# Softmax reciprocals of every chunk by way of DRAM, one matmul group kept a tile behind another, and two small matmul groups joined, in a fused attention and gated-MLP kernel

## Chip, cores, metric

One core of a Trainium2 chip. The time is the device time in microseconds (us). The profile is of one execution of each kernel (230.45 us before), and its span (first to last instruction) is about 2 us shorter than the device time.

## The reference

```python
# x: [1, 2048, 512] bf16; 32 heads of 16; window of 8 taps, dilation 2
xn = layernorm(x)
q, k, v = split(xn @ wqkv)
logits[w] = sum_d q[s] * k[s - 2*w] / 4            # 8 taps, masked for s - 2w < 0
o = sum_w softmax(logits)[w] * v[s - 2*w]
s = o @ wo
y = (gelu(xn @ w_gate) * (xn @ w_up)) @ w_down     # hidden size 1792
return x + s * silu(y)
```

## The kernel before

The 2048 positions are worked in four chunks of 512. A chunk goes through "glu" (14 slots of a gate and an up projection, 4 matmuls each), then, for the next chunk, "qkv" (12 projections of 4 matmuls), then "down" (4 tiles of 128 positions: 14 matmuls for y, 4 for s). The attention of a chunk is hung between these on a list of places: VectorE makes products q*k (`pk`), TensorE sums them to logits `L` with a 32-column operand, ScalarE takes exp (`E`), VectorE makes products E*v (`pv`), and TensorE sums them over the taps (`o`). The denominators are a small sum of E alone; their reciprocals must be spread from 32 heads to 128 partitions before `o` is divided.

```python
    def denominators(j):                # 8 matmuls, 32 columns wide
        den = mm.tile([P, P], F32, name="den_ps", tag="mm")
        ...                             # lhsT=hsum, rhs=E
        nc.vector.reciprocal(out=rs[:], in_=den[:])

    def spread_reciprocals(j):          # last chunk only: 4 matmuls and an eviction
        sp = mm.tile([P, TQ], F32, name="sp_ps", tag="mm")
        for q in range(4):
            nc.tensor.matmul(sp[:, q * P : (q + 1) * P], lhsT=spread[:, q, :],
                             rhs=st[j]["rs"][:], start=True, stop=True)
        rb = op.tile([P, TQ], F32, name="rb")
        nc.scalar.activation(out=rb[:], in_=sp[:], func=AF.Copy)

    def spread_by_dma(j):               # the other chunks: store, then four reloads
        nc.sync.dma_start(out=rs_d[j][:, :], in_=st[j]["rs"][:])
        rb = op.tile([P, TQ], BF16, name="rbd")
        for i in range(WL):
            nc.sync.dma_start(out=rb[H * i : H * (i + 1), :]..., in_=rs_d[j]...)

    def av_sums(j): ...                 # 32 matmuls, 32 columns wide: o_ps <- pv
    def divide(j): ...                  # oT <- o_ps * rb, two VectorE operations

    def down(j, tt):
        y = mm.tile(...)                # 14 matmuls
        nc.scalar.activation(out=sl[:, cols], in_=y[:], func=AF.Silu)
        s = mm.tile(...)                # 4 matmuls, lhsT = oT
        nc.vector.tensor_tensor(out=m[:], in0=s[:], in1=sl[:, cols], op=ALU.mult)
        nc.vector.tensor_tensor(out=o_t[:, cols], in0=m[:], in1=x_sb[:, t, cols], op=ALU.add)
        nc.sync.dma_start(out=out2d[...], in_=o_t[:, cols])
    ...
    # places of chunk 0's attention (cut)
    at(("qkv", 1, 3), denominators, 0)
    at(("qkv", 1, 3), spread_by_dma, 0)
    at(("qkv", 1, 10), av_sums, 0)
    at(("qkv", 1, 10), divide, 0)
    ...
    # and of the last chunk
            at(("glu", j, 12), spread_reciprocals, j)
            at(("glu", j, 13), divide, j)
```

PSUM has four rotating buffers (`mm`) and one of four banks (`att`) for L and o in turn. All DMA is issued in order from one queue.

The softmax here doesn't subtract the row's maximum and nothing guards it: scores larger than these inputs give would overflow.

## Time and profile before

| | before |
|---|---|
| median of 3 runs | 230.13 us (230.06 to 230.57) |
| profiled span | 228.7 us |
| TensorE busy | 223.6 us (98%) |
| VectorE, ScalarE, GpSimd busy | 147.6, 130.2, 23.0 us |
| granted TensorE clock | 1.000 |

A busy TensorE is not one at full rate, so this goes by start to start: the difference between two starts in the PE timeline, divided by the matmuls in between, against the 0.216 us of a full-rate stretch. The lines are in the prediction.

### The profile page before, as it was taken

How to read it: one execution, taken by the hardware profiler on the slowest of the kernel's cores; microseconds unless marked ns; L12 is line 12 of the kernel's file. 1: busy time of each engine (PE TensorE's matmuls, PEld its weight loads, DVE VectorE, ACT ScalarE, POOL GpSimd, SP SyncE). 2: the span in 40 equal slices, each digit the busy share in tenths (PEclk: the TensorE clock that was granted, in tenths of full speed). 3: DMA queues.
4: the chain of work that ended last, by engine and by line, in shares of the span. 5: the costliest groups of instructions: out<-in, count | busy, mean ns of one | idle time of the engine just before them, and what ended most of it. 6: DMA issues, size and time to landing. Idle time of an engine off the chain costs nothing.

```text
span 228.7 us, 3538 instructions
## 1 busy us (share of the span) xinstructions
PE 223.6 (98%) x1324; PEld 106.3 (46%) x1324; DVE 147.6 (65%) x234; ACT 130.2 (57%) x214; POOL 23.0 (10%) x61
## 2 busy tenths in 40 slices
PE   8899999999999999999999999999999999999993
PEld 6764444444444444444444444444444444444453
DVE  4584996896995198865677169735549429945232
ACT  4679769764413866467621786747642396748211
POOL 1048973000000000110000000000000000000000
PEclk9999999999999999999999999999999999999999
DMA  6999589982378211110275711110147800000001
GB/s 163 359 373 371 140 170 199 242 204 75 109 172 197 55 24 29 26 29 0 92 175 135 170 25 28 26 34 0 45 120 165 203 26 3 0 0 4 23 23 46
DMA packets 30545, 24.46 MB, mean 107 GB/s; under 512 B 10176, under 2 KB 30528, under 8 KB 30528
## 3 DMA queue, kind: packets, MB, share of 16 engines
q1 hardware_dynamic: 30528, 24.24, 41.9%
q8 instruction: 10, 0.16, 0.3%
q14 instruction: 7, 0.06, 0.1%
HBM read 18.61 MB, written 4.31 MB: 100 GB/s over the span
## 4 chain that ended last, share of the span: by engine, by line
PE 94%; DMA 2%; ACT 1%; SPq 1%; DVE 0%; issue 0%; DVEq 0%
PE y_ps L416 21%; PE u_ps L247 21%; PE g_ps L247 21%; PE qkv_ps L247 17%; PE s_ps L426 6%; PE L_ps L304 3%; PE o_ps L375 3%; DMA wqkv_sb<-in_A_wqkv_dram 2%; PE q_ps L247 1%; ACT L400 1%; SPq L85 1%; PE den_ps L324 0%; ACT ge L400 0%; ACT vst L271 0%; PE tr L212 0%; ACT xnT L221 0%
## 5 line engine op out<-in xcount | busy, mean ns | idle before, releaser
L247 PE MATMUL g_ps<-xnT,wg_sb 128*128 128x512 bf16 x224 | 57.6, 379 | 0.0
L247 PE MATMUL u_ps<-xnT,wu_sb 128*128 128x512 bf16 x224 | 57.5, 379 | 0.0
L416 PE MATMUL y_ps<-wd_sb,h 128*128 128x512 bf16 (+1 forms) x238 | 51.2, 366 | 0.0
L404 DVE TENSOR_TENSOR h<-ge,u 128x512 bf16<-128x512 bf16 x56 | 23.8, 425 | 37.1 <-ACT u L402 36.4
L293 DVE TENSOR_TENSOR pk<-q_sb,k_sb 128x2048 bf16<-128x2048 bf16 x32 | 37.8, 1221 | 7.0 <-ACT k_sb L268 7.0
L402 ACT ACTIVATE u<-u_ps 128x512 bf16<-128x512 f32 x56 | 33.5, 599 | 14.7 <-PE u_ps L247 14.7
L400 ACT ACTIVATE ge<-g_ps 128x512 bf16<-128x512 f32 x56 | 33.5, 599 | 14.7 <-PE g_ps L247 14.4
L247 PE MATMUL qkv_ps<-xnT,wqkv_sb 128*128 128x512 bf16 (+1 forms) x208 | 40.9, 355 | 0.0
L361 DVE TENSOR_TENSOR pv<-E,v_arr 128x2048 bf16<-128x2048 bf16 x32 | 38.6, 1216 | 0.0
L416 PEld LDWEIGHTS <-h 128*128 128x128 bf16 x238 | 23.3, 98 | 25.3
L423 ACT ACTIVATE sl<-y_ps 128x512 bf16<-128x512 f32 (+1 forms) x17 | 9.7, 572 | 44.0 <-PE y_ps L416 44.0
L247 PEld LDWEIGHTS <-wu_sb 128*128 128x128 bf16 x224 | 21.9, 98 | 26.7 <-issue 0.3
L247 PEld LDWEIGHTS <-wg_sb 128*128 128x128 bf16 x224 | 21.2, 98 | 27.1 <-issue 3.0
L247 PEld LDWEIGHTS <-wqkv_sb 128*128 128x128 bf16 x224 | 21.6, 98 | 20.2 <-DMA wqkv_sb<-in_A_wqkv_dram 0.9
L434 DVE TENSOR_TENSOR m<-s_ps,sl 128x512 bf16<-128x512 f32 (+1 forms) x17 | 11.2, 658 | 24.2 <-PE s_ps L426 24.1
L426 PE MATMUL s_ps<-wo_sb,oT 128*128 128x512 bf16 (+1 forms) x68 | 16.6, 366 | 0.0
L197 POOL TENSOR_TENSOR rstd<-rstd,mhalf 128x1 f32<-128x1 f32 x12 | 7.7, 638 | 77.4 <-DVE rstd L194 75.2
L271 ACT ACTIVATE vst<-qkv_ps 128x512 bf16<-128x512 f32 x16 | 9.6, 597 | 6.4 <-PE qkv_ps L247 6.4
L268 ACT ACTIVATE k_sb<-qkv_ps 128x512 bf16<-128x512 f32 (+1 forms) x20 | 10.2, 514 | 3.5 <-PE qkv_ps L247 3.2
L265 ACT ACTIVATE q_sb<-qkv_ps 128x512 bf16<-128x512 f32 (+1 forms) x16 | 8.7, 544 | 3.6 <-PE qkv_ps L247 3.3
L426 PEld LDWEIGHTS <-oT 128*128 128x128 bf16 x68 | 6.6, 98 | 7.2
L159 POOL COPY spread<-ident 32x32 bf16<-32x32 bf16 x16 | 9.7, 646 | 0.2
(52 smaller groups left out, 115.8 us busy)
## 6 DMA issues: line engine op xcount, KB each, us to landing
v_arr<-vT SPq DMA_DIRECT2D x16, 520.0 KB, 5.1
vT<-vst SPq DMA_DIRECT2D x16, 128.0 KB, 2.1
out_dram<-o_t SPq DMA_DIRECT2D x15, 128.0 KB, 2.3
wg_sb<-in_B_w_gate_dram SPq DMA_DIRECT2D x2, 896.0 KB, 10.9
wu_sb<-in_B_w_up_dram SPq DMA_DIRECT2D x2, 896.0 KB, 12.7
wd_sb<-in_B_w_down_dram SPq DMA_DIRECT2D x1, 1792.0 KB, 13.7
wqkv_sb<-in_A_wqkv_dram SPq DMA_DIRECT2D x3, 512.0 KB, 5.6
x_sb<-in_A_x_dram SPq DMA_DIRECT2D x3, 512.0 KB, 11.4
```

The lines of the kernel that those rows point to most:

```text
L159: nc.gpsimd.tensor_copy(out=spread[H * q : H * (q + 1), q, H * j : H * (j + 1)], in_=ident[H * q : H * (q + 1), H * q : H * (q + 1)],)
L247: nc.tensor.matmul(ps, lhsT=w[:, dk, lo : lo + P], rhs=xnT[j][:, dk, i0 : i0 + n], start=(dk == 0), stop=(dk == NC - 1),)
L268: nc.scalar.activation(out=k_sb[:, c, lo : lo + n], in_=ps, func=AF.Copy)
L293: nc.vector.tensor_tensor(out=pk[:], in0=st[j]["q"][:], in1=k_sb[:, :, off : off + TQ], op=ALU.mult)
L361: nc.vector.tensor_tensor(out=pv[:], in0=st[j]["E"][:, wh, :].unsqueeze(1).to_broadcast([P, 4, TQ]), in1=st[j]["va"][:, 4 * g : 4 * g + 4, ...
L400: nc.scalar.activation(out=ge[:], in_=g_ps[:], func=AF.Gelu_apprx_tanh)
L402: nc.scalar.activation(out=u[:], in_=u_ps[:], func=AF.Copy)
L404: nc.vector.tensor_tensor(out=h[:], in0=ge[:], in1=u[:], op=ALU.mult)
L416: nc.tensor.matmul(y[:], lhsT=st[j][fc][:, tt * P : (tt + 1) * P], rhs=wd_sb[:, fc, cols], start=(fc == 0), stop=(fc == NF - 1),)
L423: nc.scalar.activation(out=sl[:, cols], in_=y[:], func=AF.Silu)
L426: nc.tensor.matmul(s[:], lhsT=st[j]["oT"][:, g, tt * P : (tt + 1) * P], rhs=wo_sb[:, g, cols], start=(g == 0), stop=(g == NC - 1),)
L434: nc.vector.tensor_tensor(out=m[:], in0=s[:], in1=sl[:, cols], op=ALU.mult)
```

## The change

The intent: take the last spread off TensorE, make one narrow group of chunk 0 out of two, and buy time for the divides that then come later by letting s run one tile behind y.

```diff
-    at(("qkv", 1, 3), denominators, 0)
-    at(("qkv", 1, 3), spread_by_dma, 0)
-    at(("qkv", 1, 10), av_sums, 0)
-    at(("qkv", 1, 10), divide, 0)
+    at(("qkv", 1, 8), denominators, 0)
+    at(("qkv", 1, 8), av_sums, 0)
+    at(("qkv", 1, 8), store_reciprocals, 0)
+    at(("qkv", 1, 10), spread_reciprocals, 0)     # now the DRAM way, for every chunk
+    at(("down", 0, 0), divide, 0)
...
-        if j + 1 < NJ:
-            at(("glu", j, 11), spread_by_dma, j)
-            at(("qkv", j + 1, 6), divide, j)
-        else:
-            at(("glu", j, 12), spread_reciprocals, j)
-            at(("glu", j, 13), divide, j)
+        at(("glu", j, 11), store_reciprocals, j)
+        at(("glu", j, 11), spread_reciprocals, j)
+        at(("qkv", j + 1, 6) if j + 1 < NJ else ("down", j, 0), divide, j)
...
-            down(j, tt)                            # y, then s of the same tile
+                sl = down(j, tt, cols)             # y
+                if todo:
+                    finish(*todo.pop())            # s of the tile before
+                if last:
+                    finish(j, tt, cols, sl)
+                else:
+                    todo.append((j, tt, cols, sl))
```

Cut: the constant `spread` and its 17 GpSimd instructions go; chunk 0's av products start one slot earlier; three products q*k of chunk 1 move ahead of chunk 0's y; `sl`, the silu of y, which now has to outlive the next y, gets three buffers in place of two.

More of the change, by code (lines that the diff above doesn't have):

```diff
@@ L81 @@
     vT = dram.tile([D, SV], BF16, name="vT")
-    rs_d = [dram.tile([P, P], BF16, name=f"rs_d{j}") for j in range(NJ - 1)]
+    rs_d = [dram.tile([P, P], BF16, name=f"rs_d{j}") for j in range(NJ)]
     def load_x(t, n=1):
@@ L140 @@
     hsum = const.tile([P, H], BF16, name="hsum")
-    spread = const.tile([P, 4, P], BF16, name="spread")
     dsum = const.tile([P, NC, H], BF16, name="dsum")
@@ L155, in sum_constants @@
             )
-        nc.gpsimd.memset(spread[:], 0.0)
-        for q in range(4):
-            for j in range(4):
-                nc.gpsimd.tensor_copy(
-                    out=spread[H * q : H * (q + 1), q, H * j : H * (j + 1)],
-                    in_=ident[H * q : H * (q + 1), H * q : H * (q + 1)],
-                )
     xnT = {}
@@ L334, in denominators, with store_reciprocals @@
         st[j]["rs"] = rs
+    def store_reciprocals(j):
+        nc.sync.dma_start(out=rs_d[j][:, :], in_=st[j]["rs"][:])
     def spread_reciprocals(j):
-        sp = mm.tile([P, TQ], F32, name="sp_ps", tag="mm")
-        for q in range(4):
-            nc.tensor.matmul(
-                sp[:, q * P : (q + 1) * P], lhsT=spread[:, q, :], rhs=st[j]["rs"][:],
-                start=True, stop=True,
-            )
-        rb = op.tile([P, TQ], F32, name="rb")
-        nc.scalar.activation(out=rb[:], in_=sp[:], func=AF.Copy)
-        st[j]["rb"] = rb
-    def spread_by_dma(j):
-        nc.sync.dma_start(out=rs_d[j][:, :], in_=st[j]["rs"][:])
-        rb = op.tile([P, TQ], BF16, name="rbd")
+        rb = op.tile([P, TQ], BF16, name="rb")
         for i in range(WL):
@@ L405, in glu @@
         st[j][fc] = h
-    def down(j, tt):
-        t = j * TPQ + tt
-        halves = [slice(0, D // 2), slice(D // 2, D)] if t == NT - 1 else [slice(0, D)]
-        n = D // len(halves)
-        sl = sm2.tile([P, D], BF16, name="sl")
-        o_t = sm4.tile([P, D], BF16, name="o_t")
-        for i, cols in enumerate(halves):
-            y = mm.tile([P, n], F32, name="y_ps", tag="mm")
-            for fc in range(NF):
-                nc.tensor.matmul(
-                    y[:],
-                    lhsT=st[j][fc][:, tt * P : (tt + 1) * P],
-                    rhs=wd_sb[:, fc, cols],
-                    start=(fc == 0),
-                    stop=(fc == NF - 1),
-                )
-            nc.scalar.activation(out=sl[:, cols], in_=y[:], func=AF.Silu)
-            s = mm.tile([P, n], F32, name="s_ps", tag="mm")
-            for g in range(NC):
-                nc.tensor.matmul(
-                    s[:],
-                    lhsT=st[j]["oT"][:, g, tt * P : (tt + 1) * P],
-                    rhs=wo_sb[:, g, cols],
-                    start=(g == 0),
-                    stop=(g == NC - 1),
-                )
-            m = sm2.tile([P, n], BF16, name="m")
-            nc.vector.tensor_tensor(out=m[:], in0=s[:], in1=sl[:, cols], op=ALU.mult)
-            nc.vector.tensor_tensor(out=o_t[:, cols], in0=m[:], in1=x_sb[:, t, cols], op=ALU.add)
-            nc.sync.dma_start(out=out2d[t * P : (t + 1) * P, cols], in_=o_t[:, cols])
@@ new lines, in down @@
+    def down(j, tt, cols):
+        n = cols.stop - cols.start
+        y = mm.tile([P, n], F32, name="y_ps", tag="mm")
+        for fc in range(NF):
+            nc.tensor.matmul(
+                y[:],
+                lhsT=st[j][fc][:, tt * P : (tt + 1) * P],
+                rhs=wd_sb[:, fc, cols],
+                start=(fc == 0),
+                stop=(fc == NF - 1),
+            )
+        sl = sm.tile([P, n], BF16, name="sl")
+        nc.scalar.activation(out=sl[:], in_=y[:], func=AF.Silu)
+        return sl
@@ new lines, in finish @@
+    def finish(j, tt, cols, sl):
+        t, n = j * TPQ + tt, cols.stop - cols.start
+        s = mm.tile([P, n], F32, name="s_ps", tag="mm")
+        for g in range(NC):
+            nc.tensor.matmul(
+                s[:],
+                lhsT=st[j]["oT"][:, g, tt * P : (tt + 1) * P],
+                rhs=wo_sb[:, g, cols],
+                start=(g == 0),
+                stop=(g == NC - 1),
+            )
+        m = sm2.tile([P, n], BF16, name="m")
+        nc.vector.tensor_tensor(out=m[:], in0=s[:], in1=sl[:], op=ALU.mult)
+        o_t = sm4.tile([P, n], BF16, name="o_t")
+        nc.vector.tensor_tensor(out=o_t[:], in0=m[:], in1=x_sb[:, t, cols], op=ALU.add)
+        nc.sync.dma_start(out=out2d[t * P : (t + 1) * P, cols], in_=o_t[:])
@@ L462 @@
     for i in range(8):
-        at(("glu", 0, 12 + i) if i < 2 else ("qkv", 1, (0, 1, 3, 4, 5, 6)[i - 2]),
+        at(("glu", 0, 11 + i) if i < 3 else ("qkv", 1, (0, 1, 2, 4, 5)[i - 3]),
            av_product, 0, i // 2, i % 2)
-    at(("qkv", 1, 3), denominators, 0)
-    at(("qkv", 1, 3), spread_by_dma, 0)
-    at(("qkv", 1, 10), av_sums, 0)
-    at(("qkv", 1, 10), divide, 0)
+    at(("qkv", 1, 8), denominators, 0)
[3 more added lines that the diff above has]
+    at(("down", 0, 0), divide, 0)
     for j in range(1, NJ):
         for w in range(W):
-            early = j > 1 and w < 3
-            at(("qkv", j, 9 + w) if early else ("down", j - 1, w // 3), qk_product, j, w)
+            at(("qkv", j, 9 + w) if w < 3 else ("down", j - 1, w // 3), qk_product, j, w)
         for i in range(TPQ):
@@ L538 @@
                 qkv(j + 1, i)
+        todo = []
         for tt in range(TPQ):
             run("down", j, tt)
-            down(j, tt)
+            last = j * TPQ + tt == NT - 1
+            for cols in (slice(0, D // 2), slice(D // 2, D)) if last else (slice(0, D),):
+                sl = down(j, tt, cols)
[5 more added lines that the diff above has]
+                    todo.append((j, tt, cols, sl))
+        if todo:
+            finish(*todo.pop())
 _INS = ['A_x', 'A_wqkv', 'A_wo', 'B_x', 'B_w_gate', 'B_w_up', 'B_w_down']
```

## The prediction

> **What bounds the kernel now.** I read the page first (busy shares, slices, chain), then the timeline of the TensorE, then the other engines' timelines around each instruction that moves. Busy shares and the chain of the page:
>
> ```profile
> PE 223.6 (98%) x1324; PEld 106.3 (46%) x1324; DVE 147.6 (65%) x234; ACT 130.2 (57%) x214; POOL 23.0 (10%) x61
> PE   8899999999999999999999999999999999999993
> ...
> PEclk9999999999999999999999999999999999999999
> ...
> PE 94%; DMA 2%; ACT 1%; SPq 1%; DVE 0%; issue 0%; DVEq 0%
> ```
>
> The TensorE (PE) is busy in every slice but the first two and the last, its clock is full, and 94% of the chain that ended last is PE. Busy is no proof of full rate, so I look at start to start in the PE timeline (start, duration, line, operation, count). These are chunk 0's attention among the projections of chunk 1, the same place in chunk 1 itself, the projections of chunk 2, and the spread in the last chunk:
>
> ```profile
> 44.75 2.75 PE L247 MATMUL qkv_ps<-xnT,wqkv_sb 128*128 128x512 bf16 x12
> 47.43 0.29 PE L324 MATMUL den_ps<-E,hsum 128*32 128x128 bf16 x8
> 47.66 6.22 PE L247 MATMUL qkv_ps<-xnT,wqkv_sb 128*128 128x512 bf16 x28
> 53.80 1.91 PE L375 MATMUL o_ps<-pv,hsum 128*32 128x512 bf16 x32
> 55.65 1.90 PE L247 MATMUL qkv_ps<-xnT,wqkv_sb 128*128 128x512 bf16 x8
> 57.38 3.18 PE L416 MATMUL y_ps<-wd_sb,h 128*128 128x512 bf16 x14
> 60.41 1.03 PE L426 MATMUL s_ps<-wo_sb,oT 128*128 128x512 bf16 x4
> 61.27 3.18 PE L416 MATMUL y_ps<-wd_sb,h 128*128 128x512 bf16 x14
> ...
> 93.00 1.03 PE L247 MATMUL u_ps<-xnT,wu_sb 128*128 128x512 bf16 x4
> 93.96 0.29 PE L324 MATMUL den_ps<-E,hsum 128*32 128x128 bf16 x8
> 94.08 1.90 PE L375 MATMUL o_ps<-pv,hsum 128*32 128x512 bf16 x32
> 95.91 1.04 PE L247 MATMUL g_ps<-xnT,wg_sb 128*128 128x512 bf16 x4
> ...
> 101.10 10.52 PE L247 MATMUL qkv_ps<-xnT,wqkv_sb 128*128 128x512 bf16 x48
> 111.46 3.19 PE L416 MATMUL y_ps<-wd_sb,h 128*128 128x512 bf16 x14
> ...
> 205.80 0.39 PE L339 MATMUL sp_ps<-rs,spread 128*128 128x128 bf16 x4
> 206.02 1.03 PE L247 MATMUL g_ps<-xnT,wg_sb 128*128 128x512 bf16 x4
> ```
>
> From 101.10 to 111.46 there are 48 matmuls: 10.36/48 = 0.216 us each. y takes 60.41 - 57.38 = 3.03 = 14 x 0.216, s takes 61.27 - 60.41 = 0.86 = 4 x 0.216. So PE runs y, s, y, s with no hole: s already finds its divided operand oT ready, and nothing in this pair is waiting today. Apart from the first 7 us and one hole of 0.2 us at 21.2 (ScalarE loading a table), the only PE time that is not streaming is about 0.1 us wherever the width of the stationary operand changes (128 to 32 columns or back): 55.65 - 53.80 is 1.85 for work that, four narrow matmuls side by side, streams in 8 x 0.216 = 1.73.
>
> **What the Trainium skill says.** "TensorE: Matmul & The Clock Gate", section "Wait — 56ns, not 53.3ns?": 512 columns back to back take 215.7 ns on a warm array; the trace's 0.216 us agrees, so these stretches have nothing left to give but instructions. "TensorEngine Tiling (Array Packing)", "Key Properties": changing the tiling mode drains the engine; the trace agrees with the 0.1 us above. "DMA: Bandwidth & Descriptors", "Anatomy of one DMA — SWDGE (gpsimd) path": a fixed cost of some 2.0 us per transfer, mostly waiting for the write to be confirmed. That fit is for another issuing path; in this trace the 32 KB stores of reciprocals land in 1.5 us (median) and their reloads in 1.7 us, so it is near, and the measured ones are used. "SBUF — State Buffer", "Who interferes with whom": a VectorE (DVE) operation with two SBUF inputs shuts out a GpSimd instruction that reads SBUF. The trace agrees: the 32x32 copies into `spread`, beside DVE's products, average 646 ns, the same copies into `hsum`, with DVE idle, 204 ns.
>
> **The change, part by part.**
>
> (1) The last chunk's spread goes by way of DRAM. It takes 4 matmuls off PE: 206.02 - 205.80 = 0.22 us, on the path, saved. It also takes one 0.59 us eviction off ScalarE and 17 instructions (9.7 + 0.5 = 10.2 us, 21 to 31.5 us) off GpSimd. ScalarE waits for PE before nearly every eviction at that place, GpSimd's next job comes at 33 us, and DVE's products took 1.22 us beside the copies and after them: off the path, worth 0. What it adds is a latency. In the last chunk the reciprocal ends at 203.25 + 0.95 = 204.2; store 1.5, four issues of 0.43, landing 1.7 of the last: about 204.2 + 1.5 + 1.3 + 1.7 = 208.7, 209 with the hand-overs. The divide now stands behind the last h product instead of before it: u of that product was evicted at 209.74 + 0.60, now 0.22 earlier, so h is done near 210.5. The two divides, 2.35 together, end at 212.9. s of tile 0 follows two y: 209.26 + 6.04 = 215.3. Slack 2.4 us: hidden.
>
> (2) Denominators of chunk 0 joined to the sums. Both use the same narrow operand, so one pair of changes of width goes. Apart: from 44.75 to 47.66 less 12 matmuls is 2.91 - 2.59 = 0.32, and 47.66 to 55.65 less 28 is 7.99 - 6.04 = 1.95; together 2.27. Joined, as in chunk 1: 93.00 to 95.91 less 4 matmuls is 2.91 - 0.86 = 2.05. Saved: 0.22 us on the path.
>
> (3) s one tile behind y. The same 14- and 4-matmul groups in another order, all 128 wide: 0 on PE. It loosens s's need of oT by 3.0 us in each chunk, which today nobody waits for. It serves to pay for (1) and for chunk 0's later divide. The tail stays y half, s half, m, o_t, store. Tile 2's s now ends 2.4 us before the end of PE, and its two DVE steps (0.69 + 0.42) and the first half's (0.42 + 0.29) fit in that: 1.82. So 0.
>
> (4) The sums of chunk 0 come two projections earlier, the av products one slot earlier, three products qk of chunk 1 earlier. This is the place to check; the DVE timeline in chunk 0:
>
> ```profile
> 43.30 1.22 DVE L361 TENSOR_TENSOR pv<-E,v_arr 128x2048 bf16<-128x2048 bf16 x1
> ...
> 49.65 0.95 DVE L333 RECIPROCAL rs<-den_ps 128x128 bf16<-128x128 f32 x1
> 50.51 3.43 DVE L361 TENSOR_TENSOR pv<-E,v_arr 128x2048 bf16<-128x2048 bf16 x3
> 55.77 2.36 DVE L387 TENSOR_TENSOR oT<-o_ps,rbd 128x1024 bf16<-128x1024 f32 x2 [1.83 <-PE o_ps L375]
> ```
>
> DVE runs without a hole from 42.6 to the last av product at 50.51 + 3.43 = 53.94. In the changed order the reciprocal (50.51 - 49.65 = 0.86) comes after it instead, so it ends at 53.08. PE reaches the sums after 8 projections: 44.75 + 32 x 0.216 = 51.66, denominators until 51.87, sums from there, eight steps of 0.216; the last product is needed at 51.87 + 7 x 0.216 = 53.38. Slack 0.3 us less a hand-over of 0.1: the narrowest point of the change.
>
> Chunk 0's divide: the reciprocal ends at 53.95, its store has landed at 55.6; the queue issues two stores of v in between (they wait for their evictions, to about 56.2), then four reloads to 58.4, the last landing near 59.7. The divide runs from 59.8 to 62.2. y starts at 57.16, so s of tile 0 starts at 57.16 + 6.04 = 63.2. Slack 1.0 us. After it DVE has five products and two m/o_t pairs, 5 x 1.14 + 2 x 1.05 = 7.8: 70.0, and the logits want the products at about 72.6.
>
> Sum: 0.22 + 0.22 = 0.44; 230.13 - 0.44 = 229.7.
>
> **Rivals.**
> (a) The sums of chunk 0 wait for the last av product. For: slack is 0.2 to 0.3 us, in an estimate as coarse as that. Against: the products' pace is steady to 0.01 us, and v_arr's last part lands at 30.1 + 12.1 = 42.2, before the earlier start of 42.96. If it misses by 0.2 to 0.5, half or all of the gain goes: 229.9 to 230.2.
> (b) Chunk 0's reloads of the reciprocals come late, because they queue behind stores of v (in the kernel before, two of those took 4 us to land when they stood behind the reloads). At 2 us later s would wait about 1 us: 230.7. Against: the v stores are issued 0.4 us or more ahead and are single ones.
> (c) The order y, y, s matters after all, because a PSUM buffer, ScalarE or DVE is freed sooner: 229.0 or less. Against: PE shows no hole at any y or s in the kernel before. A hole that does not exist cannot be filled.
> (d) The stores at the end bunch up (three within 2 us instead of 3.6) and the last one lands later by a few tenths: 229.9. Against: each is at most 128 KB and they are issued over 1 us apart or nearly so.
>
> **Range and chances.** All four rivals but (c) lead upwards by tenths, and the before runs themselves lie from 230.06 to 230.57. So 229.7, eight times in ten within 229.3 to 230.3. Two per cent is 4.6 us; only 0.44 us of work is removed, and no wait stands on PE that could give the rest: faster by over 2% has 1%. Slower by over 2% would need (b) several times over: 1%. Within 2%: 98%.
>
> **What would show it.** PE's timeline: no spread matmuls in the last chunk and its first y about 0.44 us earlier than 209.48; denominators and sums of chunk 0 in a row and y of chunk 0 near 57.16 instead of 57.38, a saving that stays constant until the last chunk. PE busy falls by about 0.4 us, instructions by 8 PE ones in all counting weight loads. A wait of PE for a pv or oT, which the kernel before does not have, would show (a) or (b); a first divide of chunk 0 later than 62 us, or a step in the saving at 63 us, would name (b). A saving above 0.7 us would mean that I overlooked a wait in the y and s pairs; a shorter PE but the same span would be (d).

## The result, and the profile after

229.75 us, median of 6 runs (229.62 to 229.99), against 230.12 us, median of 6 runs of the kernel before (229.93 to 230.57). The ratio is 0.9981, 95% interval 0.9968 to 0.9994: faster by 0.2%. (A ratio here is worked out from the fast runs of both kernels; it is not quite the ratio of the medians.)

The PE timeline of the changed kernel, same places as in the prediction (start, duration, line, operation, count):

```profile
44.54 7.07 PE L238 MATMUL qkv_ps<-xnT,wqkv_sb 128*128 128x512 bf16 x31
51.54 0.29 PE L315 MATMUL den_ps<-E,hsum 128*32 128x128 bf16 x8
51.66 1.90 PE L357 MATMUL o_ps<-pv,hsum 128*32 128x512 bf16 x32
53.49 3.63 PE L238 MATMUL qkv_ps<-xnT,wqkv_sb 128*128 128x512 bf16 x15
56.96 6.21 PE L394 MATMUL y_ps<-wd_sb,h 128*128 128x512 bf16 x28
63.00 1.03 PE L410 MATMUL s_ps<-wo_sb,oT 128*128 128x512 bf16 x4
...
204.51 1.03 PE L238 MATMUL u_ps<-xnT,wu_sb 128*128 128x512 bf16 x4
205.37 1.03 PE L238 MATMUL g_ps<-xnT,wg_sb 128*128 128x512 bf16 x4
...
208.83 5.99 PE L394 MATMUL y_ps<-wd_sb,h 128*128 128x512 bf16 x27
214.87 1.03 PE L410 MATMUL s_ps<-wo_sb,oT 128*128 128x512 bf16 x4
```

Denominators and sums stand in a row, two y follow one another, the spread is gone, and no line has a bracket with a wait. (Counts such as x31 are a record lost: the program has 32 there, and in all 20 of its 1320 matmuls are missing from this trace. Hence PE busy, 222.4 us against 223.6, must not be compared; the starts can.)

Cut at landmarks of the PE timelines, the two kernels differ in three stages and agree within 0.01 us in the rest. "Logits" is the start of L of that chunk; the experiments are cut in the same way, each entry a difference of two starts.

| stage of PE, us | before | after | e1 | e2 | e3 | e5 | e6 | e7 | e8 | e9 |
|---|---|---|---|---|---|---|---|---|---|---|
| first q to logits 0 | 27.26 | 27.17 | 27.24 | 27.17 | 27.25 | 27.17 | 27.17 | 27.17 | 27.04 | 27.17 |
| logits 0 to first y of chunk 0 | 23.12 | 22.91 | 23.13 | 22.90 | 22.91 | 23.12 | 24.42 | 23.13 | 22.90 | 22.90 |
| first y to logits 1 | 15.64 | 15.63 | 15.63 | 17.50 | 15.63 | 15.64 | 15.64 | 15.63 | 15.64 | 16.32 |
| logits 1 to logits 3 | 108.15 | 108.15 | 108.15 | 108.15 | 108.15 | 108.59 | 108.15 | 108.15 | 108.15 | 108.15 |
| logits 3 to first y of chunk 3 | 28.31 | 28.09 | 28.31 | 28.08 | 28.31 | 28.30 | 28.08 | 28.09 | 28.08 | 28.08 |
| first y of chunk 3 to end of PE | 15.75 | 15.74 | 15.75 | 15.95 | 15.75 | 15.75 | 15.75 | 15.74 | 15.75 | 15.75 |
| start of first q | 7.00 | 6.88 | 6.97 | 6.89 | 7.06 | 7.09 | 6.64 | 6.61 | 6.89 | 6.58 |

The joined sums give 23.12 - 22.91 = 0.21, the spread 28.31 - 28.09 = 0.22: 0.43 us. The spans of the two profiles differ by more, 0.7 us, and the rest is not the change's. The first q starts anywhere from 6.58 to 7.09 us over the ten profiles, kernels that are the same up to there included, and the first stage has two values, 27.17 or about 27.25, by the wait that comes before the first q. The short ones have this line (one of six alike), the others have waited longer (0.5 to 0.7 us), on a DMA or with another name in the bracket:

```profile
6.88 1.91 PE L238 MATMUL q_ps<-xnT,wqkv_sb 128*128 128x256 bf16 x16 [0.24 <-ACT xnT L212]
```

So about 0.2 us between these two profiles (7.00 - 6.88, and 27.26 - 27.17) is the start of that execution. It is also of the size of the scatter between runs of one kernel, and the reason to trust stages, not spans, for differences of a few tenths.

Where the time that the change bought was spent, in the VectorE timeline of chunk 0:

```profile
42.44 1.22 DVE L343 TENSOR_TENSOR pv<-E,v_arr 128x2048 bf16<-128x2048 bf16 x1
...
46.85 5.76 DVE L343 TENSOR_TENSOR pv<-E,v_arr 128x2048 bf16<-128x2048 bf16 x5
52.53 0.95 DVE L324 RECIPROCAL rs<-den_ps 128x128 bf16<-128x128 f32 x1
...
59.94 2.36 DVE L369 TENSOR_TENSOR oT<-o_ps,rb 128x1024 bf16<-128x1024 f32 x2 [3.12 <-DMA rb<-rs_d]
```

The last av product ends at 46.85 + 5.76 = 52.61. PE wants it at 51.66 + 7 x 0.216 = 53.17: it has 0.56 us of room. The divide waits 3.12 us for the reloads of the reciprocals (in the kernel before it waited 1.83 us there, for its sums and not for the reloads), and ends at 62.30, against s at 63.00. VectorE pays the wait, TensorE does not.

### The profile page after: what moved, and what is told of

Its sections match the earlier page's. It is cut to its first block, busy times and chain, and to the rows that moved or that the text cites. A ratio compares the mean times of both kernels' runs of the same rounds, so it can differ in the third digit from the quotient of the medians.

```text
span 228.0 us, 3495 instructions
## 1 busy us (share of the span) xinstructions
PE 222.4 (98%) x1300; PEld 106.8 (47%) x1320; DVE 147.6 (65%) x234; ACT 129.8 (57%) x213; POOL 12.8 (6%) x44
## 4 chain that ended last, share of the span: by engine, by line
PE 95%; ACT 2%; issue 1%; DVE 0%; ACTq 0%; DVEq 0%
PE u_ps L238 21%; PE y_ps L394 21%; PE g_ps L238 19%; PE qkv_ps L238 17%; PE s_ps L410 6%; PE L_ps L295 3%; PE o_ps L357 3%; PE warm_ps L220 2%; PE q_ps L238 1%; ACT u L384 1%; ACT L382 1%; PE tr L203 1%; PE den_ps L315 0%; ACT xnT L212 0%; ACT ge L382 0%
## 5 line engine op out<-in xcount | busy, mean ns | idle before, releaser
L238 PE MATMUL g_ps<-xnT,wg_sb 128*128 128x512 bf16 x213 | 56.3, 379 | 0.4
L394 PE MATMUL y_ps<-wd_sb,h 128*128 128x512 bf16 (+1 forms) x236 | 50.2, 366 | 0.1
L410 PE MATMUL s_ps<-wo_sb,oT 128*128 128x512 bf16 (+1 forms) x66 | 15.8, 366 | 0.2
L369 DVE TENSOR_TENSOR oT<-o_ps,rb 128x1024 bf16<-128x1024 f32 x8 | 9.4, 1216 | 3.1 <-DMA rb<-rs_d 3.1
```

The source lines that it names most:

```text
L238: nc.tensor.matmul(ps, lhsT=w[:, dk, lo : lo + P], rhs=xnT[j][:, dk, i0 : i0 + n], start=(dk == 0), stop=(dk == NC - 1),)
L394: nc.tensor.matmul(y[:], lhsT=st[j][fc][:, tt * P : (tt + 1) * P], rhs=wd_sb[:, fc, cols], start=(fc == 0), stop=(fc == NF - 1),)
L410: nc.tensor.matmul(s[:], lhsT=st[j]["oT"][:, g, tt * P : (tt + 1) * P], rhs=wo_sb[:, g, cols], start=(g == 0), stop=(g == NC - 1),)
```

## The experiments

### e1: the lag alone

```diff
 # kernel before; shortened, the last tile as in the change
-            down(j, tt)
+            sl = down(j, tt, cols); if todo: finish(*todo.pop()); todo.append(...)
```

> The kernel before with s one tile behind y and nothing else. My theory: the same matmuls in another order, so no change: within 0.1 us of the kernel before, PE start to start from the first y of a chunk to the logits of the next chunk equal to before (15.64 us in chunk 0), ratio 1.000. The rival that y, y, s frees a PSUM buffer or an engine sooner: 0.4 us faster or more, with these stretches shorter.

Measured: 230.38 us, ratio to before 1.0002 (0.9990 to 1.0015). Every stage is as before (first y to logits: 15.63 against 15.64). The order y, y, s, y is worth nothing by itself: TensorE did not wait at s before, so there was no hole to fill.

### e2: the changed kernel without the lag

```diff
 # changed kernel
-                if todo:
-                    finish(*todo.pop())
-                ...
+                finish(j, tt, cols, sl)
```

> The changed kernel with s again straight behind its own y. My theory: the lag is what hides the later divides. In chunk 0 s of tile 0 would be due 3.02 us after the first y, at 59.98, but the divides end at 61.1 and 62.3, so PE waits about 1.9 us there; in the last chunk the second divide ends at 212.4 where s wants it at 212.3, so 0.1 to 0.3 us more. Together 2.0 to 2.2 us slower than the changed kernel, about 231.8, with a wait of s for oT in the PE timeline. The rival, that the lag is mere order and the divides are early enough: no slower than the changed kernel by more than 0.3 us.

Measured: 232.12 us (231.63 to 233.21), ratio 1.0086 (1.0064 to 1.0108): slower than the kernel before. The PE timeline, with the waits in brackets:

```profile
56.96 3.19 PE L394 MATMUL y_ps<-wd_sb,h 128*128 128x512 bf16 x14
61.14 0.60 PE L410 MATMUL s_ps<-wo_sb,oT 128*128 128x512 bf16 x2 [0.99 <-DVE oT L369]
62.27 0.60 PE L410 MATMUL s_ps<-wo_sb,oT 128*128 128x512 bf16 x2 [0.53 <-DVE oT L369]
62.71 3.19 PE L394 MATMUL y_ps<-wd_sb,h 128*128 128x512 bf16 x14
```

s, due at 59.98, gets its first two matmuls at 61.14 and its last two at 62.27, each after its half of the divide: 17.50 - 15.63 = 1.87 us in chunk 0 and 15.95 - 15.74 = 0.21 in the last, 2.08 together, as expected. This is what the lag pays for. (The brackets count from the modelled end of the matmul before, so they sum to less.)

### e3: the last chunk's spread on TensorE again

```diff
 # changed kernel; the constant and the matmuls of the kernel before put back
-        at(("glu", j, 11), store_reciprocals, j)
-        at(("glu", j, 11), spread_reciprocals, j)
+        if j + 1 < NJ: (as above)
+        else: at(("glu", j, 12), spread_on_pe, j)
```

> The changed kernel with the reciprocals of the last chunk spread by four matmuls on PE again, as before, and its constants made on GpSimd again. My theory: 0.22 us slower than the changed kernel (between it and the kernel before), all of it at the four matmuls in PE's timeline, nothing before them. If the GpSimd copies mattered by way of VectorE or DMA, the stages before the last chunk would be longer too, and the loss would be more than 0.3 us.

Measured: 230.07 us, ratio to before 0.9992 (0.9981 to 1.0004). One stage moves, the one with the spread: 28.31 against 28.09, 0.22 us. The 17 GpSimd instructions that came back lengthen no stage of TensorE beyond that.

They do lengthen a wait of VectorE. Ahead of chunk 0's av products VectorE waits for a small GpSimd operation of the layernorm (`rstd`). The wait is 0.73 to 0.75 us in the three kernels that make `spread` (before, e1, e3) and 0.44 us in the seven that do not; first the kernel before, then the changed one:

```profile
42.63 0.41 DVE L203 TENSOR_SCALAR xn<-x_sb,mv,rstd 128x512 bf16<-128x512 bf16 x1 [0.75 <-POOL rstd L197]
```

```profile
42.11 0.41 DVE L194 TENSOR_SCALAR xn<-x_sb,mv,rstd 128x512 bf16<-128x512 bf16 x1 [0.44 <-POOL rstd L188]
```

In e3 the last av product ends at 53.16 and TensorE wants it at 51.92 + 7 x 0.216 = 53.43: 0.27 us of room, where the changed kernel has 0.56. So the copies are off TensorE's path, but they take half of the room at the narrowest place of the change. Why GpSimd starts `rstd` later there, some 10 us after the last copy, is not shown.

### e5: denominators apart from the sums in all four chunks

```diff
 # changed kernel
-    at(("qkv", 1, 8), denominators, 0)
+    at(("qkv", 1, 6), denominators, 0)
...
-        at(("glu", j, 11), denominators, j)
+        at(("glu", j, 8), denominators, j)
```

> The changed kernel with the denominators taken out of the pair in all four chunks (two projections earlier in chunk 0, three slots earlier in the others), so that each pays its own change of operand width. The order on VectorE stays the same in chunk 0. My theory: 4 x 0.21 = 0.85 us slower than the changed kernel, 230.6, in four steps of 0.2 us in PE's start times. If joining saves nothing on PE and the measured gain was chance: within 0.2 us of the changed kernel.

Measured: 230.78 us, ratio to before 1.0020 (1.0007 to 1.0033). The four steps are there: 23.12 - 22.91 = 0.21 in chunk 0, 108.59 - 108.15 = 0.44 in chunks 1 and 2, 28.30 - 28.09 = 0.21 in chunk 3; 0.86 together. The PE timeline of chunk 1 shows what one costs:

```profile
87.82 1.03 PE L238 MATMUL u_ps<-xnT,wu_sb 128*128 128x512 bf16 x4
88.78 0.29 PE L315 MATMUL den_ps<-E,hsum 128*32 128x128 bf16 x8
89.00 1.04 PE L238 MATMUL g_ps<-xnT,wg_sb 128*128 128x512 bf16 x4
```

From 87.82 to 89.00 are 1.18 us for 4 wide matmuls (0.86) and 8 narrow ones: 0.32 for the group. In the joined pair the same 8 take 51.66 - 51.54 = 0.12. The 0.2 in between is the extra change of width into the narrow group and out of it.

### e6: chunk 0's sums two projections earlier still

```diff
 # changed kernel
-    at(("qkv", 1, 8), denominators, 0)     # and av_sums, store_reciprocals
+    at(("qkv", 1, 6), denominators, 0)     # and av_sums, store_reciprocals
```

> The changed kernel with chunk 0's denominators and sums two projections earlier still (after the sixth instead of the eighth). My theory: VectorE's last av products are the limit: its last one ends at 52.6 in the changed kernel's trace, PE would want it at 49.95 + 7 x 0.216 = 51.5, so PE waits for the last products and everything after is 0.9 to 1.1 us later, about 230.7. That would show that the place chosen by the change has about half a microsecond of room and no more. If something else feeds the sums late or they have more room than I think: under 0.3 us slower.

Measured: 231.29 us, ratio to before 1.0046 (1.0032 to 1.0060). The stage grew by 24.42 - 22.91 = 1.51 us, more than I had expected. Its PE timeline, and then its VectorE timeline:

```profile
51.58 0.40 PE L357 MATMUL o_ps<-pv,hsum 128*32 128x512 bf16 x4 [0.42 <-DVE pv L343]
52.71 0.40 PE L357 MATMUL o_ps<-pv,hsum 128*32 128x512 bf16 x4 [0.73 <-DVE pv L343]
```

```profile
42.48 1.23 DVE L343 TENSOR_TENSOR pv<-E,v_arr 128x2048 bf16<-128x2048 bf16 x1 [0.21 <-DMA v_arr<-vT]
...
46.90 5.76 DVE L343 TENSOR_TENSOR pv<-E,v_arr 128x2048 bf16<-128x2048 bf16 x5
```

The wait is where the theory has it: sums 7 and 8 wait for the last two av products. Of the miss, part is my arithmetic: from the changed kernel's starts, PE wants the last product at 44.54 + 24 x 0.216 + 0.22 + 7 x 0.216 = 51.45 and had its sum released at 52.7, so 1.25 and not 0.9 to 1.1. The rest is this execution. TensorE started 6.88 - 6.64 = 0.24 us earlier than in the changed kernel's profile, but VectorE could not follow: its first av product waited 0.21 us for the load of v, and its last ended at 52.66, the same clock time as before (52.61). So the room of 0.56 us in the changed kernel's profile is not fixed. By the same sum it is 0.56 us in e2, 0.44 in e5, 0.27 in e9 and 0.10 in e8. In e5, e8 and e9, as here, the first av product waited 0.20 to 0.37 us for the load of v; in the changed kernel and e2 it did not wait. What sets when v lands was not found. An early start of TensorE alone does not decide it: e5, with the latest start (7.09), waited 0.23 us.

### e7: the way by DRAM alone, without the lag

```diff
 # kernel before; the spread constant and matmuls removed
+        at(("glu", j, 11), spread_by_dma, j)      # for every j
+        at(("qkv", j + 1, 6) if j + 1 < NJ else ("glu", j, 13), divide, j)
```

> The kernel before with only the last chunk's reciprocals spread by way of DRAM, s straight behind y, the divide where it was (ahead of the last h product). My theory: the reloads land near 208.5, the divide runs 208.6 to 211.0, h of the last slot still comes before PE's fourteenth matmul of y at 212.1, and s at 212.3 finds oT ready: so the 0.22 us are had without the lag, ratio 0.999 against before, and the lag is needed for the later sums of chunk 0 only. If the DRAM way is too slow without the lag: a PE wait in the first y or s of the last chunk of 0.3 us or more, and no gain or a loss.

Measured: 230.14 us, ratio 0.9995 (0.9982 to 1.0009); the interval does not separate 0.2 us from nothing, the stage does: 28.09 against 28.31, the whole 0.22, and the stage after it is 15.74, so s did not wait. VectorE in the last chunk:

```profile
208.44 2.36 DVE L368 TENSOR_TENSOR oT<-o_ps,rbd 128x1024 bf16<-128x1024 f32 x2
210.71 0.42 DVE L385 TENSOR_TENSOR h<-ge,u 128x512 bf16<-128x512 bf16 x1
```

The divide ends at 210.80, s began at 211.80, and the last h is there at 211.13, before TensorE's fourteenth matmul of y at 208.78 + 13 x 0.216 = 211.59. With the divide at its old place this part needs no lag.

### e9: no lag, but the reloads first in the queue

```diff
 # e2
-    at(("qkv", 1, 10), spread_reciprocals, 0)
+    at(("qkv", 1, 8), spread_reciprocals, 0)
...
-        at(("qkv", j + 1, 6) if j + 1 < NJ else ("down", j, 0), divide, j)
+        at(("qkv", j + 1, 6) if j + 1 < NJ else ("glu", j, 13), divide, j)
```

> The changed kernel without the lag, as in the run that lost 1.86 us in chunk 0 and 0.21 us in the last, but with chunk 0's reloads of the reciprocals ahead of all four stores of v in the queue, and the last chunk's divide ahead of the last h product again. My theory: what made s wait there was the place of the reloads in the queue, not the way by DRAM itself. The store of the reciprocals lands near 54.95, the reloads near 58.2, the divides run 58.3 to 60.6, and s, due at 59.98, wants their second half at 60.41: a PE wait of 0.2 us at most in chunk 0, none in the last, so within 0.3 us of the changed kernel (about 229.8 to 230.0). If the way by DRAM is too slow for this chunk wherever it stands in the queue: again 1 us or more lost between the first y and the logits of chunk 1.

Measured: 229.99 us (229.86 to 230.88), ratio to before 1.0001 (0.9985 to 1.0018). The loss in chunk 0 fell from 1.87 to 16.32 - 15.63 = 0.69 us, that in the last chunk to nothing (15.75). But I had expected 0.2 us at most. The PE timeline:

```profile
56.65 3.19 PE L394 MATMUL y_ps<-wd_sb,h 128*128 128x512 bf16 x14
59.67 0.59 PE L410 MATMUL s_ps<-wo_sb,oT 128*128 128x512 bf16 x2
60.77 0.60 PE L410 MATMUL s_ps<-wo_sb,oT 128*128 128x512 bf16 x2 [0.51 <-DVE oT L369]
```

The second half of the divide ended at 58.36 + 2.36 = 60.72, near the 60.6 that I had worked out; s wanted it at 59.67 + 0.43 = 60.10 and not at 60.41. TensorE started 0.3 us earlier in this execution (6.58, against 6.89 in e2) and VectorE did not follow: its first av product again waited 0.20 us for v. Against e2 the divide ended (59.85 + 2.36) - 60.72 = 1.49 us earlier, and s was due 59.98 - 59.67 = 0.31 us earlier: 1.87 - 1.49 + 0.31 = 0.69. Most of e2's loss in chunk 0, 1.49 of 1.87 us, was therefore the reloads' place behind two stores of v in the queue, and not the way by DRAM. With e2's start some 0.4 us would be left (an estimate from these numbers, not run). The lag covers both: in the changed kernel the second half of the divide, which s wants two matmuls after its start, has 63.00 + 0.43 - 62.30 = 1.13 us to spare.

### e8: gelu's table loaded earlier

The one hole in the middle of TensorE's work, 0.2 us at 21.0, is in both kernels.

```diff
 # changed kernel, ahead of the evictions of v of chunk 0
+    nc.scalar.preload_act_table(AF.Gelu_apprx_tanh)
```

> The changed kernel with the table for gelu loaded on ScalarE ahead of the four evictions of v of chunk 0, where ScalarE has time, and not ahead of the first gelu. PE shows one hole of 0.2 us at 21.0, where u of the second slot waits for a PSUM buffer that the first gelu frees. My theory: this hole closes, 0.2 us faster than the changed kernel, near 229.5. If the hole has another cause, or the later evictions of v hold PE up instead: no gain, or a hole earlier.

Measured: 229.57 us (229.50 to 230.19), ratio to before 0.9979 (0.9966 to 0.9992). In the PE timelines of the changed kernel and of this one, the u of the second slot:

```profile
19.94 1.03 PE L238 MATMUL g_ps<-xnT,wg_sb 128*128 128x512 bf16 x4
21.01 1.02 PE L238 MATMUL u_ps<-xnT,wu_sb 128*128 128x512 bf16 x4
```

```profile
20.02 1.03 PE L238 MATMUL g_ps<-xnT,wg_sb 128*128 128x512 bf16 x4
20.88 1.03 PE L238 MATMUL u_ps<-xnT,wu_sb 128*128 128x512 bf16 x4
```

21.01 - 19.94 = 1.07 became 20.88 - 20.02 = 0.86, the full rate: 0.21 us gained there. The stage shows 27.04 against 27.17 only, because this execution had the slow kind of start (0.52 us of wait before the first q, as in e1, whose stage is 27.24). This is the best of the kernels by its stages, though with the least room in chunk 0 (0.10 us, see e6). That it beats the changed kernel was seen in the trace; the two were not timed in the same rounds, and their ratios to before (0.9979 and 0.9981) do not tell them apart.

## Why the prediction was right

The predicted 229.7 us was measured as 229.75. The signs that it named came 0.2 us early: the first y of chunk 0 at 56.96 (named: 57.16), that of the last chunk at 208.83 (named: 209.48 - 0.44 = 209.04). That 0.2 us is the start of the profiled execution; the saving between is the forecast one. By its steps:

- *The bound.* TensorE at 0.216 us a matmul with no hole at y or s: confirmed by e1, where the new order alone changed no stage by over 0.02 us.
- *Part 1, the spread, 0.22 us.* Measured 0.22, alone (e7) and undone (e3). The GpSimd and ScalarE work it removes is off the path, as said: e3 brought it back and lost the 0.22 alone. But for part 4 the GpSimd copies were not worth 0: their absence gave VectorE 0.3 us, which the step overlooked. Here the reciprocal ended at 202.82 + 0.95 = 203.77, and the divide ran from 210.06 to 212.41; s came at 214.87. The slack that the step put at 2.4 us was 2.46.
- *Part 2, the joined sums, 0.22 us.* Measured 0.21, and 0.86 for four such joints (e5).
- *Part 3, the lag, 0.* Right (e1). What the step said it buys is shown by e2: without it 2.08 us are lost. One thing it did not say: for the last chunk the lag is needed only because the change also moved the divide behind the last h (e7).
- *Part 4, the narrow place.* It was put at 0.3 us less a hand-over of 0.1, and was 0.56 in this profile. The sum was right for the kernel it was read from, in which GpSimd still makes `spread` (0.27 in e3); without those copies VectorE's wait for GpSimd ahead of the av products is 0.44 us in place of 0.75. The divide was put at 59.8 to 62.2 and ran from 59.94 to 62.30.
- *Rivals.* (a), the sums waiting for the av products, did not come true here, but e6 shows that it is the next thing to happen; its counter-argument, that v lands in time, holds by a few tenths only, and not always (e5, e6, e8 and e9 waited 0.20 to 0.37 us for v). (b), late reloads, did not come true either: the divide began 0.14 us after the forecast. Its mechanism is real, though: e9 shows that standing behind the stores of v costs 1.49 us; the forecast had counted that, and the lag hid it. (c) is refuted by e1. (d), bunched stores, did not come: the span ends 3.4 us after PE's modelled end (228.0 and 224.6), before 3.5 us (228.7 and 225.2).

What the prediction left out was the start: it took the first 7 us as equal, and they differ by up to half a microsecond between executions. The stated range covered that; a gain of 0.43 us is close to the limit of what six runs can show.

## What to carry to other kernels

When one engine streams without holes, only instructions taken from it, or changes of operand width saved, shorten the kernel; reordering its work is worth nothing in itself, but it can pay for a latency elsewhere, so price the two together. When work is moved to a transfer, look at what stands before it in the queue: here that made 1.49 of the 1.87 us that chunk 0 lost without the lag. For gains of tenths of a microsecond cut the traces at landmarks and compare stages: they repeat to 0.01 or 0.02 us where the times of one kernel's runs scatter by half a microsecond.

## What the Trainium skill lacked or had wrong

- "TensorEngine Tiling (Array Packing)", "Key Properties", says that a change of tiling mode drains the engine, without a figure: here one excursion from 128 columns to 32 and back costs 0.2 us beside its own matmuls (0.86 us for four, e5).
- "TensorE: Matmul & The Clock Gate", "Back-to-back issue gap", gives about 131 ns a matmul of 512 columns as the sustained rate of load and matmul pairs, and calls the 216 ns of the formula too high for a stream. Here the streams of such pairs that were measured took 216 ns each (48 in 10.36 us), every matmul with its own weight load; the section "Wait — 56ns, not 53.3ns?" of the same page has it right.
- "DMA: Bandwidth & Descriptors", "Anatomy of one DMA — SWDGE (gpsimd) path", has a fixed cost of some 2.0 us fitted on the GpSimd path; for the sync engine's path the page gives the delay of the first byte, but no such fit. For 32 KB from the sync engine's queue the traces show 1.4 to 1.5 us to DRAM and 1.7 to 2.0 us back (medians by place).
- No page that I read gives the scatter of a kernel's start: here the first matmul that needs loaded weights began between 6.58 and 7.09 us over ten profiles of the same opening.
